# The first six attention tiles computed from key and query columns, one decay table, and another order of loads

## The chip, the cores and the metric

The kernel runs on one core of one Trainium2 chip. The metric is the device time of one execution in microseconds, the median of three runs. A profile of one further execution is read beside it.

## The reference, cut to what matters

Three layers follow each other, all in float32:

```python
# r, k, v: (4, 8, 768, 48); w, u: (8, 48)
for t in range(768):
    cur = einsum('bhd,bhe->bhde', u * k[t], v[t])
    y[t] = einsum('bhd,bhde->bhe', r[t], state + cur)
    state = w[:, :, None] * state + einsum('bhd,bhe->bhde', k[t], v[t])
x = y as (3072, 384)
h = x @ w_in                      # (384, 2048)
x = (h - tanh(h)) @ w_out         # (2048, 384)
# top-1 mixture of 8 experts: cosine logits against expert_emb over tau,
# softmax weight of the best expert, relu(x @ w1[e]) @ w2[e]
```

## The kernel before, in words

The 3072 tokens are 24 attention tiles of 128 tokens. Tile n is batch n % 4, piece n // 4 of its sequence, so tiles 0 to 3 are the first pieces of the four batches (no state goes in) and tiles 4 and 5 second pieces. Three tiles make one token group of 384; group j passes the FFN in 16 steps f of 128 hidden units. All large products are made as three float32r products of high and low parts.

An attention tile (class Att, lines 317 to 429) has its operands twice: r and k as columns (RT and KT, 112 x 4 x 128, tile `tt`: two heads of 48 stacked at partitions 0 and 64) and r, k and v as rows (128 tokens; v padded to 512 columns). The host lays both out. Steps of a tile: `decay_r` and `decay_k` multiply RT and KT by the tables tab_r and tab_k (powers of w, and inverse powers). `bonus` makes r*k*u from the rows in two GpSimd operations, `sums` reduces it over each head's 48 numbers on VectorE into cd. `diagonal` puts cd on the diagonals of two masks `am` (8 ScalarE operations on the identity). `scores` multiplies KT by RT on TensorE, 16 products. `causal` copies the scores above the diagonal into `am` on VectorE. `values` multiplies v and am on TensorE (32 products), `result` splits the outcome into high and low parts of the FFN's input xt (ScalarE, VectorE). `decayed` multiplies the key rows by ktab on GpSimd, a table by rows that `decay_rows` turns out of tab_k; `state_product` and `state_add` make the state for the next tile of the batch.

The weights of the FFN, 64-bit floats in memory, come in 16 pieces of 768 KB in the order w_in, w_out, w_in, ... Each is packed to float32 on VectorE by six bit operations (`convert`, lines 228 to 255) and then split by ScalarE (high) and GpSimd (low) in `split` (line 257). A piece of w_in serves two FFN steps. Pieces of w_out also give router columns: `Logits.turn` (turns by TensorE), `product`, `back`. A raw piece lies in one of seven buffers (STAGE, line 208); `load_next` asks for the next piece once its buffer's previous user is done. Every load is issued on SyncE's one queue, in order.

The startup (lines 137 to 1158) is ordered by hand: inside `manual_schedule` the instructions keep the written order on each engine. There tiles 0 to 2 are computed and pieces 0 to 2 packed. After it comes a loop over 22 steps (lines 1211 to 1258): FFN steps 0 to 5 of group 0, then all 16 of group 1. In the meantime tiles 3 to 5 are made (`attention_stage`, begun at steps 0, 1 and 2) and the remaining pieces packed (at the steps of CONV). From there on a planner with its own cost estimates orders the instructions, and it may also put instructions of the loop between those of the startup. A second part finishes group 0 and does groups 2 to 7 with their tiles, and the experts follow. `store_x` writes a group's columns to memory for a rare path; `routing_table` initializes a table in memory; `embedding_norms`, `embedding_rows`, `embedding_columns` normalize the expert embeddings (a power on GpSimd, then VectorE, then a turn).

PSUM has eight banks, one pool for all tiles named `ps`.

```python
a[2].causal()                        # startup, line 1134
a[2].values()
a[1].result()
ops = convert_next()
for i in range(2):
    for _ in range(3):
        next(ops)
    split(*ready[0], i=i)
```

Of the kernel before, what the change touches and what calls it, by code (L numbers as in the profile page):

```python
# [24 lines left out]
LZ = 0.04  # L25
# [4 lines left out]
def rwkv__then__tanh_ffn__then__top1_moe_kernel(  # L30
# [55 lines left out]
    CONV = (1, 2, 3, 5, 6, 7, 8, 9, 11, 12, 13, 15, 18)  # L86
# [52 lines left out]
    wc = const.tile([PW, HP, 1], F32, name="wc")  # L139
    nc.vector.memset(wc, 0.5)  # L140
# [21 lines left out]
    nc.vector.tensor_copy(out=tri16, in_=strict)  # L162
    sb_t = const.tile([P, 1], F32, name="sb_t")
    nc.vector.memset(sb_t, SB)
    lz_t = const.tile([P, 1], F32, name="lz_t")
    nc.vector.memset(lz_t, -LZ)
    half = const.tile([P, TB], F32, name="half")
    nc.vector.memset(half, 0.5)
    zx = const.tile([P, NB * NF], F32, name="zx")
    ent = const.tile([P, NK, EP], F32, name="ent")  # L170
    nc.vector.memset(ent, 0.0)
# [4 lines left out]
    pw = const.tile([PW, HP, 8], F32, name="pw")  # L176
    w64 = pw[:, :, 6:7]
    w128 = pw[:, :, 7:8]
    rw64 = const.tile([PW, HP, 1], F32, name="rw64")
# [3 lines left out]
    def decay_tables():  # L183
        nc.vector.tensor_copy(out=pw[:, :, 0:1], in_=wc)
        for i in range(7):
            nc.vector.tensor_tensor(out=pw[:, :, i + 1:i + 2], in0=pw[:, :, i:i + 1], in1=pw[:, :, i:i + 1],
                                    op=ALU.mult)
        nc.vector.reciprocal(out=rw64, in_=w64)
        nc.vector.tensor_copy(out=tab_r[:, :, 0:1], in_=rw64)
        nc.vector.tensor_copy(out=tab_k[:, :, P - 1:P], in_=rw64)  # L190
        for i in range(7):
            n = 1 << i
            f = pw[:, :, i:i + 1].to_broadcast([PW, HP, n])
            nc.vector.tensor_tensor(out=tab_r[:, :, n:2 * n], in0=tab_r[:, :, 0:n], in1=f, op=ALU.mult)
            nc.vector.tensor_tensor(out=tab_k[:, :, P - 2 * n:P - n], in0=tab_k[:, :, P - n:P], in1=f, op=ALU.mult)

    def decay_rows():
        pse = ps.tile([P, HP, PW], F32, tag="p", name="ps_tab")
        for q in range(HP):
            nc.tensor.transpose(pse[:, q, :], tab_k[:, q, :], ident[:PW, :PW])  # L200
        for g in range(2):
            nc.scalar.activation(out=ktab.rearrange("p (q g) d -> p g q d", g=2)[:, g],
                                 in_=pse[:, :, 64 * g:64 * g + D], func=AF.Copy)


    CW = 2 * P

# [9 lines left out]
    def load_win(c, t):  # L217
        t = t.rearrange("p (k f) -> p k f", k=NK)
        cols = slice(c * CW, (c + 1) * CW)
        nc.sync.dma_start(out=t, in_=w_in.rearrange("(k p) f -> p k f", p=P)[:, :, cols])  # L220
# [1169 lines left out]
```

## Time and profile before

| | |
|---|---|
| median of 3 runs | 821.34 us (819.63 to 821.76) |
| profiled execution | 822.99 us, span 821.3 us |
| TensorE busy | 775.1 us, 94% |
| VectorE / ScalarE / GpSimd busy | 512.1 / 446.6 / 301.8 us |
| mean granted clock of TensorE | 0.963 |

The span is the profiled time from the first instruction to the last; the execution has 1.7 us around it. A matmul's end is modelled, so a busy TensorE is not one at its peak. The granted clock is a share of 2.4 GHz: 0.50 is 1.2 GHz.

### The profile page before, as it was taken

Reading aid. Unit: us, or ns where it says so; the run is one execution under the profiler, and the core shown is the slowest. Engines: PE = TensorE matmul, PEld = TensorE weight load, DVE = VectorE, ACT = ScalarE, POOL = GpSimd, SP = SyncE. Lnnn points to the kernel's source line nnn. Section 1 sums busy time; section 2 is a strip of 40 time slices with the busy share of each in tenths; the row PEclk is TensorE's granted clock in tenths of the full one; section 3 lists DMA queues with packets and bytes.
Section 4 is the critical chain, followed back from the end, with each engine's and each line's share of the span. In section 5 each row is a group of like instructions: output and inputs, shape, how many; then the busy total and the mean of one; then the engine's idle time right before and its main releaser. Section 6 shows DMA issues by size and latency. Waiting matters only on the chain. (4 is left out here: it accounts for less than half of the span.)

```text
span 821.3 us, 15368 instructions
## 1 busy us (share of the span) xinstructions
PE 775.1 (94%) x5835; PEld 726.9 (89%) x5835; DVE 512.1 (62%) x1092; ACT 446.6 (54%) x1032; POOL 301.8 (37%) x311
## 2 busy tenths in 40 slices
PE   6579999989999999999999999999899999999992
PEld 3468989879999999999989999998889999999992
DVE  6887977666865776775766784756544445454510
ACT  3356676645566656656547666776343434544421
POOL 6563461176541551551561440142331314331111
PEclk7759999999999999999999999999989999999996
DMA  8862621133222222223213201150633335544300
GB/s 275 267 200 94 225 89 39 53 88 114 85 77 91 86 62 106 85 59 111 84 56 113 84 2 58 32 182 30 194 129 121 125 116 185 172 153 152 116 28 30
DMA packets 41446, 89.69 MB, mean 109 GB/s; under 512 B 9329, under 2 KB 21025, under 8 KB 40339
## 3 DMA queue, kind: packets, MB, share of 16 engines
q1 hardware_dynamic: 37042, 79.10, 29.6%
q0 software_dynamic: 4320, 9.51, 3.6%
q8 instruction: 48, 0.79, 0.5%
q14 instruction: 36, 0.29, 0.1%
HBM read 69.82 MB, written 19.47 MB: 109 GB/s over the span
## 5 line engine op out<-in xcount | busy, mean ns | idle before, releaser
L475 PE MATMUL ph<-xt,wq 128*128 128x384 f32 (+2 forms) x1712 | 346.4, 345 | 3.0 <-DVE glo L540 2.5
L475 PEld LDWEIGHTS ph<-xt,wq 128*128 128x128 f32 x1712 | 307.7, 191 | 8.1 <-DVE glo L540 3.4
L486 PE MATMUL acc<-wq,ghi 128*128 128x392 f32 (+2 forms) x1120 | 288.1, 344 | 0.2 <-ACT ghi L553 0.2
L486 PEld LDWEIGHTS acc<-wq,ghi 128*128 128x128 f32 (+1 forms) x1120 | 200.3, 187 | 6.5 <-issue 1.4
L486 PE MATMUL acc<-wq,glo 128*128 128x392 f32 (+2 forms) x560 | 184.9, 342 | 0.5 <-DVE glo L540 0.5
L524 ACT ACTIVATE z<-ph 128x384 f32<-128x384 f32 x128 | 62.6, 489 | 86.2 <-PE ph L475 84.8
L486 PEld LDWEIGHTS acc<-wq,glo 128*128 128x128 f32 (+1 forms) x560 | 103.9, 187 | 1.9 <-DVE glo L540 0.8
L535 ACT ACTIVATE ghi<-ph 128x384 fp32r<-128x384 f32 x128 | 62.6, 490 | 70.2 <-DVE ph L534 62.9
L533 DVE TENSOR_TENSOR ph<-ph,z 128x384 f32<-128x384 f32 x128 | 71.7, 561 | 40.8 <-ACT z L524 40.4
L540 DVE TENSOR_TENSOR glo<-ph,ghi 128x384 fp32r<-128x384 f32 x128 | 71.0, 555 | 41.1 <-ACT ghi L535 39.9
L709 POOL DMA_INDIRECT out_dram<-ob,gts x27 | 28.7, 1063 | 155.1 <-ACT ob L787 149.6
L525 ACT ACTIVATE q<-z,sb_t 128x384 f32<-128x384 f32 x128 | 78.9, 617 | 3.5
L534 DVE SCALAR_TENSOR_TENSOR ph<-q,ph 128x384 f32<-128x384 f32 x128 | 71.7, 561 | 11.3 <-ACT q L525 2.5
L554 DVE SCALAR_TENSOR_TENSOR glo<-ph,ghi 128x384 fp32r<-128x384 f32 (+2 forms) x56 | 31.5, 564 | 74.7 <-ACT ghi L553 65.4
L537 ACT ACTIVATE mk<-z,lz_t 128x384 bf16<-128x384 f32 x128 | 77.1, 602 | 0.0
L553 ACT ACTIVATE ghi<-ph 128x384 fp32r<-128x384 f32 (+2 forms) x56 | 27.7, 496 | 72.8 <-PE ph L475 70.7
L756 DVE TENSOR_TENSOR wq<-eraw,wq 128x768 fp32r<-128x768 f32 x60 | 55.5, 964 | 18.5 <-ACT wq L755 16.9
L755 ACT ACTIVATE wq<-eraw 128x768 fp32r<-128x768 f32 x64 | 50.5, 837 | 12.9 <-DMA eraw<-in_moe_w_dram 12.9
L340 POOL TENSOR_TENSOR rk<-rkv 128x384 f32<-128x384 f32 x22 | 22.6, 1026 | 94.0 <-DMA xs<-xr 64.6
L259 POOL TENSOR_TENSOR wq<-wraw,wq 128x768 fp32r<-128x768 f32 (+1 forms) x17 | 30.2, 1774 | 45.2 <-ACT wq L258 45.2
L332 POOL TENSOR_TENSOR tt<-tt,tab_k 112x512 f32<-112x512 f32 x20 | 34.4, 1721 | 26.5 <-DMA tt<-in_cols_dram 21.3
L355 POOL TENSOR_TENSOR am<-ident,cd 128x512 f32<-128x512 f32 x36 | 36.9, 1047 | 10.6 <-DVE cd L345 10.6
(270 smaller groups left out, 891.4 us busy)
## 6 DMA issues: line engine op xcount, KB each, us to landing
eraw<-in_moe_w_dram SPq DMA_DIRECT2D x32, 768.0 KB
rkv<-in_rows_dram SPq DMA_DIRECT2D x22, 640.0 KB
tt<-in_cols_dram SPq DMA_DIRECT2D x22, 448.0 KB
xd<-xt SPq DMA_DIRECT2D x8, 1152.0 KB
wraw<-in_moe_w_in_dram SPq DMA_DIRECT2D x8, 768.0 KB
wraw<-in_moe_w_out_dram SPq DMA_DIRECT2D x8, 768.0 KB
xs<-xr SPq DMA_DIRECT2D x21, 192.0 KB
first<-in_rows_dram SPq DMA_DIRECT2D x1, 640.0 KB
```

The source lines that it names most:

```text
L355: nc.gpsimd.tensor_tensor(out=a, in0=ident[:, None, :].to_broadcast([P, HP, P]), in1=self.cd[:, :, g:g + 1].to_broadcast([P, HP, P]), op=A ...
L475: nc.tensor.matmul(out=ph, lhsT=lhs[a][:, kk, :], rhs=rhs(b, kk), start=(kk == 0 and p == 0), stop=(kk == nk - 1 and p == 2))
L486: mm = nc.tensor.matmul(out=acc[t], lhsT=g[a][:, t * P:t * P + m], rhs=rhs(b, i), start=(i == span[0] and p == 0), stop=(i == span[1] - 1 ...
L524: nc.scalar.activation(out=z, in_=ph, func=AF.Square)
L525: nc.scalar.activation(out=q, in_=z, func=AF.Square, scale=SS, bias=sb_t)
L533: nc.vector.tensor_tensor(out=ph, in0=ph, in1=z, op=ALU.mult)
L534: nc.vector.scalar_tensor_tensor(out=ph, in0=q, scalar=KC, in1=ph, op0=ALU.add, op1=ALU.mult)
L535: mark["z"] = nc.scalar.activation(out=ghi, in_=ph, func=AF.Copy).ins
L537: nc.scalar.activation(out=mk, in_=z, func=AF.Relu, bias=lz_t, accum_out=zx[:, step:step + 1])
L540: nc.vector.tensor_tensor(out=glo, in0=ph, in1=ghi.bitcast(F32), op=ALU.subtract)
L755: nc.scalar.activation(out=hi[c][:, a], in_=t[:, a], func=AF.Copy)
L756: engs[s % len(engs)].tensor_tensor(out=lo[c][:, a], in0=t[:, a], in1=hi[c][:, a].bitcast(F32), op=ALU.subtract)
```

## The change

For tiles 0 to 5 only v is loaded as rows (256 KB in place of 640 KB). r*k comes from the columns in one operation (`products`: VectorE for tiles 0 to 2, GpSimd for 3 to 5), before the decays; `summed` multiplies it on TensorE by `u_pair`, u as columns with zeros for the other head, and ScalarE copies the sums to cd. The decayed key rows come from the decayed columns: `turned` turns them on TensorE into a bank, `turned_rows` copies them out on ScalarE. Tiles 6 to 23 are as before. tab_k is no longer built by doublings: ScalarE copies tab_r backwards. w goes straight into the table of powers; w and u are asked for on ScalarE's queue.

Loads on SyncE: tiles 0, 1, 2, the embedding and tau, then five weight pieces, then tiles 3, 4, 5, then u as rows. Before: tile 0, u, embedding, tau, tiles 1, 2, three pieces, the routing table, tile 3, a fourth piece, tile 4, further pieces, tile 5. `store_x` and `routing_table` now come behind the last weight load asked for by then (the mark before was a ScalarE instruction, which a load on SyncE doesn't follow). In the startup the clears of the state tiles, the embedding's norms, the constants and the routing's iotas come after tiles 0 to 2; piece 2 is packed in the loop's step 0 instead of the startup.

```diff
-    CONV = (1, 2, 3, 5, 6, 7, 8, 9, 11, 12, 13, 15, 18)
+    CONV = (0, 1, 2, 3, 5, 6, 7, 8, 9, 11, 12, 13, 15, 18)
...
     for g in range(2):
-        nc.sync.dma_start(out=wc[64 * g:64 * g + D, :, 0],
-                          in_=w.rearrange("(q g) d -> g d q", g=2)[g])
+        nc.scalar.dma_start(out=pw[64 * g:64 * g + D, :, 0], in_=w.rearrange("(q g) d -> g d q", g=2)[g])
+    for g in range(2):
+        nc.scalar.dma_start(out=u_pair[64 * g:64 * g + D, :, g], in_=u.rearrange("(q g) d -> g d q", g=2)[g])
...
+        for i in range(6):
+            square(i)
+        nc.vector.reciprocal(out=tab_r[:, :, 0:1], in_=w64)
         for i in range(7):
             n = 1 << i
-            f = pw[:, :, i:i + 1].to_broadcast([PW, HP, n])
-            nc.vector.tensor_tensor(out=tab_r[:, :, n:2 * n], in0=tab_r[:, :, 0:n], in1=f, op=ALU.mult)
-            nc.vector.tensor_tensor(out=tab_k[:, :, P - 2 * n:P - n], in0=tab_k[:, :, P - n:P], in1=f, op=ALU.mult)
+            if i == 5:
+                between()
+            nc.vector.tensor_tensor(out=tab_r[:, :, n:2 * n], in0=tab_r[:, :, 0:n],
+                                    in1=pw[:, :, i:i + 1].to_broadcast([PW, HP, n]), op=ALU.mult)
+        nc.scalar.activation(out=tab_k, in_=tab_r[:, :, ::-1], func=AF.Copy)
+        square(6)
...
+            if n < 2 * TB:
+                rows = rows[:, :HP * P] if n < TB else rows[:, RKV - HP * P:]
         nc.sync.dma_start(out=tt, in_=cols_in[n])
-        nc.sync.dma_start(out=rows, in_=rows_in[n * P:n * P + P, :])
+        nc.sync.dma_start(out=rows, in_=rows_in[n * P:n * P + P, (2 * DM if n < 2 * TB else 0):])
...
+        def turned(self):
+            pse = ps.tile([P, HP, P], F32, tag="p", name="ps_k")
+            for q in range(HP):
+                nc.tensor.transpose(pse[:, q, :PW], self.KT[:, q, :], ident[:PW, :PW])
+            self.pk = pse
+
+        def turned_rows(self):
+            self.ktok = work.tile([P, H, D], F32, name="ktok")
+            nc.scalar.activation(out=self.ktok, in_=self.pk.rearrange("p q (g d) -> p (q g) d", g=2)[:, :, :D],
+                                 func=AF.Copy)
+
+        def products(self, eng):
+            i = self.n % 2 + 1
+            self.rkc = rows5[:PW, i * HP * P:(i + 1) * HP * P].rearrange("p (q t) -> p q t", q=HP)
+            eng.tensor_tensor(out=self.rkc, in0=self.RT, in1=self.KT, op=ALU.mult)
+
+        def summed(self):
+            pc = ps.tile([P, HP, 2], F32, tag="p", name="ps_cd")
+            for q in range(HP):
+                nc.tensor.matmul(out=pc[:, q, :], lhsT=self.rkc[:, q, :], rhs=u_pair[:, q, :], start=True, stop=True)
+            self.cd = work.tile([P, HP, 2], F32, name="cd")
+            nc.scalar.activation(out=self.cd, in_=pc, func=AF.Copy)
...
     def store_x(j, xt):
-        with tc.issue_after(mark["z"]):
+        with tc.issue_after(mark["w"]):
...
     def routing_table():
-        for i in range(2):
+        with tc.issue_after(mark["w"]):
+            for i in range(2):
...
+    for n in range(TB):
+        load_rkv(n)
     nc.sync.dma_start(out=en, in_=emb)
     nc.sync.dma_start(out=tau_t, in_=tau.to_broadcast([P, 1]))
-    load_rkv(1)
-    load_rkv(2)
-    load_next(3)
+    load_next(5)
```

The startup after the loads, as it now stands (its lines of the diff joined):

```python
decay_tables(lambda: a[0].products(nc.vector))
a[0].summed(); a[0].decay_r(nc.vector); a[0].decay_k(nc.vector)
a[0].scores(range(HP)); a[0].diagonal(True); a[0].turned()
a[1].products(nc.vector); a[1].decay_r(nc.vector); a[1].decay_k(nc.vector)
a[1].summed(); a[1].scores(range(HP)); a[1].diagonal(True); a[1].turned()
a[0].causal(); a[0].values()
a[2].products(nc.vector); a[2].decay_r(nc.vector); a[2].decay_k(nc.vector)
a[2].summed(); a[2].scores(range(HP))
a[1].causal(); a[0].result()
a[2].diagonal(True); a[2].turned()
a[1].values()
load_rkv(3); load_rkv(4); load_rkv(5)
# u as rows, small_constants(), two packing steps of piece 0
a[2].causal(); a[2].values()
# one packing step, first half's split
a[1].result()
# three packing steps, second half's split
a[2].result()
a[0].turned_rows(); a[1].turned_rows()
for x in st:
    nc.gpsimd.memset(x, 0.0)
a[0].state_product(); a[1].state_product()
embedding_norms(); embedding_rows(); embedding_columns()
decay_rows(); load_next()
convert_now(); split(*ready[1])
a[2].turned_rows()
nc.vector.tensor_copy(out=tri16, in_=strict)
routing_constants()
```

In `attention_stage` tiles 3 to 5 do `products` and `decay_k` on GpSimd in their first stage, then `summed`, `scores`, `turned`, `diagonal` and `turned_rows` in the second; `decayed` is gone.

## Rows read from the trace of the kernel before

**Rows 1.** The page's slices, forty over the whole span: TensorE's busy tenths

```profile
PE   6579999989999999999999999999899999999992
```

**Rows 2.** Windows: stretch, length, busy us (instructions) by engine; clock, DMA share, GB/s

```profile
10.00:15.00 5.00, 3.02 (x20) 2.44 (x20) 1.98 (x5) 3.37 (x12) 0.75 (x2) 0.50 1.02 349
...
20.00:25.00 5.00, 5.00 (x84) 4.19 (x86) 3.58 (x6) 3.67 (x13) 2.61 (x3) 0.63 0.70 229
...
45.00:50.00 5.00, 2.56 (x28) 1.79 (x28) 2.07 (x4) 3.69 (x10) 2.45 (x3) 0.76 0.82 273
...
60.00:150.00 90.00, 89.53 (x688) 79.44 (x689) 70.03 (x151) 60.72 (x149) 32.80 (x22) 0.97 0.32 104
```

**Rows 3.** In order of time, VectorE, start to 33: start us, busy us, what

```profile
3.83 1.38 DVE L186 TENSOR_TENSOR pw<-pw 112x4 f32<-112x4 f32 x7
...
7.06 0.42 DVE L194 TENSOR_TENSOR tab_r<-tab_r,pw 112x256 f32<-112x256 f32 x1
...
9.14 1.48 DVE L332 TENSOR_TENSOR tt<-tt,tab_k 112x512 f32<-112x512 f32 x1
...
10.54 0.54 DVE L345 TENSOR_REDUCE cd<-rk 128x8 f32<-128x384 f32 x1
...
14.16 0.67 DVE L329 TENSOR_TENSOR tt<-tt,tab_r 112x512 f32<-112x512 f32 x1
...
18.43 1.33 DVE L371 COPY_PREDICATED am<-cmask,pa 128x512 f32<-128x512 uint8 x2
...
27.64 0.55 DVE L245 TENSOR_SCALAR bits<-wraw 128x384 int32<-128x384 int32 x1
...
32.02 0.56 DVE L402 TENSOR_TENSOR xt<-py,xt 128x384 fp32r<-128x384 f32 x1 [0.99 <-ACT xt L401]
```

**Rows 4.** In order of time, TensorE's matmuls, start to 128

```profile
10.67 2.08 PE L366 MATMUL pa<-tt 48*128 48x128 f32 x16 [3.14 <-DVE tt L332]
...
12.68 1.01 PE L200 MATMUL ps_tab<-ident,tab_k 112*128 112x112 f32 x4
...
19.26 2.58 PE L396 MATMUL py<-am,rkv 128*32 128x128 f32 x32 [1.69 <-issue]
...
23.78 1.08 PE L396 MATMUL py<-am,rkv 128*32 128x128 f32 x32
...
35.22 2.81 PE L475 MATMUL ph<-xt,wq 128*128 128x384 f32 x9
...
44.90 1.16 PE L366 MATMUL pa<-tt 48*128 48x128 f32 x16
...
60.03 3.25 PE L475 MATMUL ph<-xt,wq 128*128 128x384 f32 x9 [0.27 <-ACT wt L274]
...
127.94 0.63 PE L272 MATMUL pt<-ident,wraw 128*128 128x128 f32 x4
```

**Rows 5.** In order of time, GpSimd and ScalarE, start to 52

```profile
2.14 1.63 POOL L1103 MEMSET st<- 128x384 f32 x4
...
3.73 1.98 POOL L1080 IOTA tokid<- 128x2 int32 x24
...
11.11 2.45 ACT L353 ACTIVATE am<-ident,cd 128x128 f32<-128x128 f32 x8 [8.92 <-DVE cd L345]
...
14.31 1.57 POOL L1056 TENSOR_TENSOR en_n<-en_n,half 8x1 f32<-8x1 f32 x1 [4.25 <-DVE en_n L1055]
...
31.97 1.01 POOL L259 TENSOR_TENSOR wq<-wraw,wq 128x384 fp32r<-128x384 f32 x1
...
40.46 0.92 ACT L258 ACTIVATE wq<-wraw 128x768 fp32r<-128x768 f32 x1 [1.73 <-DVE wraw L251]
...
47.87 1.78 POOL L332 TENSOR_TENSOR cols<-cols,tab_k 112x512 f32<-112x512 f32 x1 [2.55 <-DMA cols<-in_cols_dram]
...
49.60 1.86 POOL L259 TENSOR_TENSOR wq<-wraw,wq 128x768 fp32r<-128x768 f32 x1
```

**Rows 6.** Waits of SyncE's queue, 0 to 65: in total us, times, longest

```profile
SPq L310 <- PE pst L410: 12.5, 2, 10.6
```

More of the change, by code (lines that the diff above doesn't have):

```diff
@@ L197, in decay_rows @@
+        nc.scalar.activation(out=tab_k, in_=tab_r[:, :, ::-1], func=AF.Copy)
+        square(6)
     def decay_rows():
-        pse = ps.tile([P, HP, PW], F32, tag="p", name="ps_tab")
+        pse = ps.tile([P, HP, P], F32, tag="p", name="ps_tab")
         for q in range(HP):
[L200 to L203, printed above, removed]
+            nc.tensor.transpose(pse[:, q, :PW], tab_k[:, q, :], ident[:PW, :PW])
@@ L298, in load_rkv @@
         if n == TB - 1:
-            t = work.tile([P, 2 * HP * P + RKV], F32, name="first", tag="xt")
+            t = work.tile([P, 2 * HP * P + HP * P], F32, name="first", tag="xt")
             tt = t[:PW, :2 * HP * P].rearrange("p (a q t) -> p a q t", a=2, q=HP)
@@ L1102, in rwkv__then__tanh_ffn__then__top1_moe_kernel @@
-    for t in st:
-        nc.gpsimd.memset(t, 0.0)
-    routing_constants()
-    a[0].bonus(nc.gpsimd)
+    decay_tables(lambda: a[0].products(nc.vector))
+    a[0].summed()
     a[0].decay_r(nc.vector)
     a[0].decay_k(nc.vector)
-    a[0].sums()
+    a[0].scores(range(HP))
     a[0].diagonal(True)
-    a[0].scores(range(HP))
-    embedding_norms()
-    a[1].bonus(nc.gpsimd)
+    a[0].turned()
+    a[1].products(nc.vector)
     a[1].decay_r(nc.vector)
     a[1].decay_k(nc.vector)
-    a[1].sums()
@@ L1116, in rwkv__then__tanh_ffn__then__top1_moe_kernel @@
-    decay_rows()
+    a[1].summed()
+    a[1].scores(range(HP))
     a[1].diagonal(True)
-    a[1].scores(range(HP))
+    a[1].turned()
     a[0].causal()
     a[0].values()
-    a[2].bonus(nc.gpsimd)
+    a[2].products(nc.vector)
     a[2].decay_r(nc.vector)
     a[2].decay_k(nc.vector)
-    a[2].sums()
+    a[2].summed()
     a[2].scores(range(HP))
+    a[1].causal()
+    a[0].result()
     a[2].diagonal(True)
-    a[1].causal()
+    a[2].turned()
     a[1].values()
-    a[0].result()
-    a[1].decayed()
@@ L1131, in rwkv__then__tanh_ffn__then__top1_moe_kernel @@
-    a[1].state_product()
     load_rkv(3)
-    load_next(4)
+    load_rkv(4)
+    load_rkv(5)
+    nc.sync.dma_start(out=u_bc, in_=u.rearrange("(o h) d -> o h d", o=1).to_broadcast([P, H, D]))
+    small_constants()
+    ops = convert_next()
+    for _ in range(2):
+        next(ops)
     a[2].causal()
     a[2].values()
+    next(ops)
+    split(*ready[0], i=0)
     a[1].result()
-    ops = convert_next()
-    for i in range(2):
-        for _ in range(3):
-            next(ops)
-        split(*ready[0], i=i)
@@ L1142, in rwkv__then__tanh_ffn__then__top1_moe_kernel @@
-    done.add(0)
-    a[0].decayed()
+    for _ in ops:
+        pass
+    split(*ready[0], i=1)
+    done.add(0)
+    a[2].result()
+    a[0].turned_rows()
+    a[1].turned_rows()
+    for x in st:
+        nc.gpsimd.memset(x, 0.0)
     a[0].state_product()
-    load_rkv(4)
-    load_next()
-    load_rkv(5)
-    a[2].result()
+    a[1].state_product()
+    embedding_norms()
     embedding_rows()
     embedding_columns()
+    decay_rows()
+    load_next()
     convert_now()
     split(*ready[1])
-    a[2].decayed()
@@ L1154, in rwkv__then__tanh_ffn__then__top1_moe_kernel @@
-    a[1].state_add()
-    convert_now()
-    split(*ready[2])
-    done.add(2)
+    a[2].turned_rows()
+    nc.vector.tensor_copy(out=tri16, in_=strict)
+    routing_constants()
     startup.close()
@@ L1168, in attention_stage @@
             if i == first:
-                t.bonus(nc.gpsimd)
+                t.products(nc.gpsimd)
                 t.decay_k(nc.gpsimd)
@@ L1172, in attention_stage @@
             elif i == first + 1:
-                t.sums()
+                t.summed()
+                t.scores(range(HP))
+                t.turned()
                 t.diagonal(DACT)
-                t.scores(range(HP))
+                t.turned_rows()
             elif i == first + 2:
```

76 lines of the change are left out of this document (37 added, 39 removed).

## The prediction

> **What bounds the kernel now.** I read the page's slices first. TensorE is at nine tenths or more in nearly every slice except the first three [rows 1], and from 60 to 150 us it is busy 89.53 of 90 us with VectorE only 70.03 busy [rows 2]. So the long part is TensorE's own work, the sum of its matmuls, and a microsecond saved before it fills up comes off the end one for one, unless the change adds matmuls. There is no other lever: the chain of waits names only the last scatter. What can move is the start, and I read it by windows, then in order of time, engine by engine.
>
> At the start TensorE is busy 3.02 us of 10 to 15 at a granted clock of 0.50, and the clock is at 0.63 over 20 to 25, where it worked all 5 us [rows 2]. The first FFN product stands at 35.22 us, and only from 60.03 does TensorE run without gaps [rows 4]. The first product waits for two things: the third column block of the first token group (VectorE's line 402, at 32.02 for 0.56, so 32.58) [rows 3] and the second half of the first weight piece's low part (GpSimd's line 259, at 31.97 for 1.01, so 32.98) [rows 5]. Both are ends of VectorE's in-order queue: the bit packing of that weight piece does not begin before 27.64 [rows 3], because three attention tiles stand ahead of it. From 33 to 60 the packing of the next pieces goes on; there the longest hole is 45 to 50: VectorE is busy 2.07 us, idle 2.9, and GpSimd too waits there 2.55 us, for the columns of tile 5 [rows 2, 5]. That transfer is late because SyncE's queue stood 10.6 us behind one load of rows that waited for a state product [rows 6], with weight pieces and later tiles queued behind it.
>
> **The change, part by part.** My measure is the moment at which both inputs of the first product are there (32.98 now): gain A. Then the stretch to a full TensorE: gain B. Then work added to a TensorE that is already full: loss C.
>
> A, *tables*. The squares begin at 3.83 and seven took 1.38; six take 1.2, so 5.0. Reciprocal 0.2. One table instead of two: five doublings, which shrink from the largest at 0.42; I take 0.2 for each, so 6.2. The products r*k of tile 0 now stand here: one 112x512 operation without GpSimd beside it, 0.67 [rows 3], so 6.9. Two last doublings 0.7, so 7.6. The mirror is one ScalarE copy of 512 columns, a form that the trace does not show: below by half of, above by the whole of the 768-column copy at 0.92 [rows 5]; I take two thirds, 0.6, so 8.2. The decay of r runs beside it; the decay of k adds 0.67: 8.9. Now that operation ends at 9.14 + 1.48 = 10.62, because GpSimd's bonus products run beside it [rows 3]. They go, and with them the 0.54 us reduction per tile and the wait of the diagonal for them. So tile 0 is 1.7 us earlier.
>
> The loads of w and u go to ScalarE's queue, which has nothing else to do then; if a table load is put ahead of them, w lands later. I count 0 for it and leave it to the range.
>
> *Tiles 0 to 2*. Per tile VectorE now has products, two decays (3 x 0.67 = 2.0), the causal copies (1.33) and a low part (0.56) [rows 3]; ScalarE a small copy of about 0.2, the diagonal (2.45) and a high part (half of 0.92) [rows 5]; TensorE scores (2.08 at the lower clock, 1.16 at the upper), four turns of keys (1.01 lower; four of a wider form took 0.63 upper), four sums over two columns each, and values (2.58 lower with waits, 1.08 upper) [rows 4]. The sums have no row: between 0.1 and 0.66 (they load weights like the turns but stream 2 columns instead of 112); I take 0.6 lower, 0.3 upper. TensorE per tile: 6.3 lower, 3.2 upper.
>
> Walk at the upper clock: scores of tile 0 at 8.9 to 10.1; diagonal to 10.8; VectorE finishes tile 1's three operations at 10.9, copies tile 0 to 12.2, tile 2's three to 14.2, tile 1's copies to 15.5, tile 0's low part 16.1, two packing steps (0.55 each) to 17.6; tile 2's diagonal ends at 16.9, its copies at 18.9; third packing step 19.5; ScalarE's half and the high part 20.6; low part 21.1; three packing steps 22.9; split and high part 23.9; low part, and GpSimd's 1.01, 24.5. At the lower clock TensorE is the late one: scores, turns, sums, scores, turns of tiles 0 and 1 end at 15.8, values 18.0, sums and scores of tile 2 at 20.8, its diagonal at 21.9, and the same tail gives 28.6. TensorE works here with fewer pauses than it does now, so I take the middle, 26.5: A = 33.0 - 26.5 = 6.5, from 4.4 to 8.5.
>
> By the Trainium skill ("TensorE: Matmul & The Clock Gate", What's actually happening) the throttled state is the default and sustained activity releases it; the trace agrees (0.50 at 10 to 15 with pauses, TensorE busy throughout when it rises). By that rule alone I would have taken 24.5.
>
> B. Taken away: three reductions (3 x 0.54, 1.6) [rows 3], the 2.9 us hole (the columns of tile 5 are asked for right behind five weight pieces and two tiles, with no blocked load ahead), and GpSimd's bonus and key products, three operations a tile, beside which VectorE's two-input operations grow from 0.67 to 1.48. Added: the norms of the embedding now come late. Their power on GpSimd (1.57) stands behind the last split and four clears (1.63) [rows 5], so it ends near 26.5 + 3.2 = 29.7, and VectorE's packing of the second piece stands behind it. VectorE has some 2 us of other work to fill in there: a loss of 0 to 3, I take 1.5. A cast and memsets that moved here cost up to 1. Sum: 1.6 + 2.9 - 1.5 - 1 = 2. Ends: -1 if the hole only changes its place (ScalarE's or GpSimd's order then sets the pace), +5 with nothing lost.
>
> C. Turns and sums of tiles 3 to 5: 0.6 + 0.3 = 0.9 us a tile at the upper clock. Tile 3 comes before TensorE is full, two tiles after: 1.8 (0.9 to 2.7). The write of the first token group's columns and of the routing table move behind weight loads, past the loads of tiles 3 to 5 on SyncE's queue, which only gain by it, and the transfers end up where the DMA engines are mostly idle (60 to 150: share 0.32) [rows 2]: 0.
>
> Sum: 6.5 + 2 - 1.8 = 6.7. The profiled execution took 822.99 (span 821.3, so 1.7 around it), 1.65 over the median of 821.34; a difference carries over unchanged: 821.34 - 6.7 = 814.6.
>
> **The rivals.** *Everything pays*: upper clock through tiles 0 to 2, no wait for the norms: 8.5 + 5 - 0.9 = 12.6, so 808.7. For it: VectorE has the only dense queue and loses work. Against: TensorE's clock was low through 10 to 20. The page named above would make this the forecast.
>
> *TensorE becomes the bound of the start*: the clock stays low, three tiles of 6.3 us in a row, the norms cost their full wait: 4.4 - 0.5 - 1.8 = 2.1, so 819.2. For it: its clock now, and half as much small work again for it. Against: fewer pauses.
>
> *Slower: GpSimd's queue.* It must pass four clears (1.63), the power (1.57), the second piece's split (1.86), the routing constants (1.98 for 24 of 29 iotas, so near 3) and two 112x512 operations for each of tiles 3 to 5 (up to 1.78 each) before or around the third piece's split (1.86) [rows 5]. All of it ahead of that split makes 20.6 us. From 28.6 on this ends at 49.2; if it also stands, in order, for tile 5's columns as it does now (2.55) [rows 5], at 51.8 against 51.46 now. From 51.46 on it decides: the third product is then no earlier than today, the added matmuls (1.8) remain and each further wait counts: near 824. For it: this queue sets the third product now. Against: it loses the bonus work, and nothing blocks the load of those columns any more.
>
> By the Trainium skill ("SBUF — State Buffer", Who interferes with whom) a VectorE instruction with two SBUF inputs and a GpSimd one that reads SBUF exclude each other for a whole instruction; the 1.48 against 0.67 agrees, and the new products on GpSimd are of that kind, which speaks for this rival.
>
> *It does not do what it says*: the later steps' order eats what the start gives, for instance accumulation held back by banks that the turned keys occupy until late: about 821.
>
> **How the numbers follow.** Chances: forecast 0.42 (own range 812 to 817), everything pays 0.22, TensorE bound 0.18, no effect 0.09, slower 0.09. About 0.3% (2.5 us) is what a measurement tells from no change. Faster takes the first two and half of the third: 0.73. Same: the other half and no effect, 0.18. Slower 0.09. The range 807 to 820.5 leaves out some tenth on each side.
>
> **What would show it.** Right: the first line-475 product between 24 and 30; no 10 us wait on SyncE before the fourth weight piece; VectorE's two-input operations of tiles 0 to 2 near 0.67; tile 5's columns landed before 35; TensorE without gaps from about 52; some 2 us more of small matmuls after that. Wrong: a first product after 33; GpSimd's third split after 50; scores of tiles 1 and 2 waiting for TensorE at 0.50; VectorE idle for over 3 us behind the embedding's power. A time over 819 would refute the sum, one under 809 its caution on the clock and the norms.

## The result, and the profile after

The changed kernel took 829.45 us (median of five runs; 827.46 to 830.13) against 821.34 for the kernel before in the same session: ratio 1.0098 [1.0076, 1.012], slower. Timed again on another chip it was 825.19 (822.06 to 829.18) against 822.00: 1.004 [1.0016, 1.0064]. The forecast was 814.6, and its range ended at 820.5. So about 7 us were forecast as a gain and 3 to 8 came as a loss.

The profiled execution of the changed kernel took 829.45 (span 827.8, so 1.7 around it, as before). The page's slices of TensorE:

```profile
PE   8489999989999999999999999999899999999992
```

Against [rows 1] the first slice rose from 6 to 8, the second fell from 5 to 4, the third rose from 7 to 8, and the long part is as full as it was. The windows of [rows 2]:

```profile
10.00:15.00 5.00, 4.49 (x29) 4.18 (x29) 4.67 (x8) 3.19 (x10) 0.00 (x0) 0.50 1.05 387
20.00:25.00 5.00, 4.00 (x76) 3.25 (x64) 0.80 (x2) 2.88 (x10) 2.04 (x2) 1.00 1.05 300
45.00:50.00 5.00, 4.74 (x61) 4.12 (x60) 3.70 (x9) 5.00 (x12) 4.18 (x30) 1.00 0.19 34
60.00:150.00 90.00, 89.05 (x690) 78.32 (x690) 69.61 (x150) 59.72 (x147) 31.81 (x21) 0.96 0.35 118
```

From 10 to 15 TensorE and VectorE are far busier than before, and the hole from 45 to 50 is gone (VectorE 3.70 against 2.07 us): both were forecast. The reader should stop at 20 to 25: VectorE, whose queue the forecast walked through without a pause, is busy 0.80 of 5 us, while the DMA engines are full (1.05). VectorE in order of time shows why:

```profile
6.15 1.17 DVE L187 TENSOR_TENSOR pw<-pw 112x4 f32<-112x4 f32 x6 [3.88 <-DMA pw<-in_w_dram]
...
10.60 0.69 DVE L342 TENSOR_TENSOR tt<-tt,tab_k 112x512 f32<-112x512 f32 x1
...
24.20 0.69 DVE L339 TENSOR_TENSOR tt<-tt,tab_r 112x512 f32<-112x512 f32 x1 [4.87 <-POOL rows L360]
24.81 0.55 DVE L438 TENSOR_TENSOR xt<-py,xt 128x384 fp32r<-128x384 f32 x1
...
25.42 0.54 DVE L251 TENSOR_SCALAR bits<-wraw 128x384 int32<-128x384 int32 x1
28.39 0.69 DVE L339 TENSOR_TENSOR tt<-tt,tab_r 112x512 f32<-112x512 f32 x1 [2.43 <-POOL rows L360]
...
35.41 0.56 DVE L438 TENSOR_TENSOR xt<-py,xt 128x384 fp32r<-128x384 f32 x1 [0.99 <-ACT xt L437]
```

The squares start at 6.15 instead of 3.83 [rows 3], behind w. At 24.20 and 28.39 stand the decays of r (line 339) of tiles 3 and 4. They belong to the loop, not to the hand-written start, but the planner put them into VectorE's queue ahead of tile 0's low part (24.81) and between the packing steps of the first weight piece. Each overwrites columns that GpSimd's product r*k (line 360) must have read, and GpSimd waits for those columns:

```profile
22.89 1.28 POOL L360 TENSOR_TENSOR rows<-tt 112x512 f32<-112x512 f32 x1 [20.88 <-DMA tt<-in_cols_dram]
...
27.09 1.26 POOL L360 TENSOR_TENSOR rows<-tt 112x512 f32<-112x512 f32 x1 [1.06 <-DMA tt<-in_cols_dram]
...
35.08 1.02 POOL L265 TENSOR_TENSOR wq<-wraw,wq 128x384 fp32r<-128x384 f32 x1 [2.17 <-ACT wq L264]
```

The columns of tiles 3 and 4 were asked for behind five weight pieces of 768 KB. So the chain is five pieces, then columns, then GpSimd's product, then VectorE's decay, and behind that everything in VectorE's order. VectorE's two waits that matter, from 0 to 75 us (in total, times, longest):

```profile
DVE tt L339 <- POOL rows L360: 7.3, 2, 4.9
DVE pw L187 <- DMA pw<-in_w_dram: 3.9, 1, 3.9
```

Of the first of these waits 2.6 us would have passed idle anyhow: tile 0's low part, next in VectorE's order, needs ScalarE's high part, which ended at 21.96, and VectorE had nothing left since 19.34:

```profile
21.48 0.48 ACT L437 ACTIVATE xt<-py 128x384 fp32r<-128x384 f32 x1
```

Both inputs of the first product are there at 35.41 + 0.56 = 35.97 and 35.08 + 1.02 = 36.10 (32.98 before, 26.5 forecast). TensorE:

```profile
11.34 2.08 PE L402 MATMUL pa<-tt 48*128 48x128 f32 x16 [0.51 <-DVE tt L342]
13.35 1.01 PE L348 MATMUL ps_k<-ident,tt 112*128 112x112 f32 x4
14.15 1.73 PE L366 MATMUL ps_cd<-u_pair,rows 112*128 112x2 f32 x8
...
20.31 1.05 PE L366 MATMUL ps_cd<-u_pair,rows 112*128 112x2 f32 x8
...
30.23 2.53 PE L432 MATMUL py<-am,first 128*32 128x128 f32 x32 [6.23 <-DVE am L407]
...
39.22 0.45 PE L1099 MATMUL ps_en<-ident,en 8*128 8x8 f32 x3 [1.89 <-DVE en L1094]
...
40.29 3.23 PE L511 MATMUL ph<-xt,wq 128*128 128x384 f32 x9
...
52.42 1.49 PE L511 MATMUL ph<-xt,wq 128*128 128x384 f32 x7 [1.06 <-POOL wq L265]
...
62.58 1.32 PE L522 MATMUL acc<-wq,ghi 128*128 128x392 f32 x3 [0.58 <-DVE am L407]
```

Against [rows 4] the scores of tile 0 come 0.7 us later (11.34), not 1.8 earlier, and the first product at 40.29 against 35.22. The sums (line 366) are x8: four products are recorded as eight matmuls, 1.73 us at the granted clock of 0.50 and 1.05 at the upper one.

To see what of this reaches the end I follow one event through all kernels: the start of the square of the same FFN step on ScalarE (in the last two rows a high part of the experts), each kernel minus the kernel before, in their profiled executions (us; each column is one execution, and that of before took 822.99, 1.65 over its median). The repaired kernels are e1, e7, e8 timed again and e13 of the next section:

| FFN step, time before | changed | changed, other chip | order repaired | loads repaired | three repairs | three repairs and tile 5 held |
|---|---|---|---|---|---|---|
| 0, at 46.07 | -2.5 | -2.7 | -7.0 | -6.5 | -9.0 | -12.2 |
| 2, at 55.10 | -1.1 | -1.3 | -5.5 | -4.8 | -5.6 | -8.9 |
| 3, at 63.31 | +1.5 | +1.3 | -2.9 | -2.1 | -5.4 | -8.9 |
| 5, at 77.12 | +3.0 | +1.1 | -2.2 | -2.4 | -4.4 | -7.6 |
| 20, at 143.67 | +2.1 | +0.2 | -3.1 | -3.3 | -5.3 | -8.5 |
| 96, at 448.54 | +2.7 | -1.0 | -4.3 | -3.2 | -5.1 | -8.8 |
| experts, at 617.70 | +6.1 | +0.6 | -0.7 | +0.8 | -3.4 | -8.2 |
| near the end, 801.58 | +6.4 | +0.9 | -0.5 | +1.2 | -3.0 | -7.8 |

One execution against one is coarse: b1, whose time is that of the kernel before, stands at -2.6 at step 5 in the same count. So a single difference under some 3 us tells nothing; what recurs from column to column does. Each of two repairs moves step 5 by some 5 us against the changed kernel, so what they take away is made before step 5.

Two more differences recur. From step 2 to step 3 the first four columns lose 2.6 or 2.7 us, the last two 0.2 and none. In those four one decay on VectorE takes 3.57 or 3.58 us (shown below for the changed kernel, at 55.45), in the last two the longest takes 2.38 and 2.37, and the next packing, ScalarE's split and the square of step 3 stand behind it; no run tests this by itself. And 1 to 4 us are lost around 580 to 612 in most kernels of the changed family. There ScalarE's split of expert weights waits longer for them (before, then the changed kernel):

```profile
583.08 1.58 ACT L755 ACTIVATE wq<-eraw 128x768 fp32r<-128x768 f32 x2 [3.46 <-DMA eraw<-in_moe_w_dram]
```

```profile
588.37 1.58 ACT L787 ACTIVATE wq<-eraw 128x768 fp32r<-128x768 f32 x2 [5.33 <-DMA eraw<-in_moe_w_dram]
```

A high part stands behind that split in ScalarE's order, and TensorE waits 2.1 us for it (0.2 before). Why the weights land later stays open.

### The profile page after: what moved, and what is told of

Its sections match the earlier page's. It is cut to its first block, busy times and chain, and to the rows that moved or that the text cites. A ratio compares the mean times of both kernels' runs of the same rounds, so it can differ in the third digit from the quotient of the medians.

```text
span 827.8 us, 15511 instructions
## 1 busy us (share of the span) xinstructions
PE 783.1 (95%) x5907; PEld 735.1 (89%) x5907; DVE 506.7 (61%) x1080; ACT 450.4 (54%) x1044; POOL 285.1 (34%) x296
## 5 line engine op out<-in xcount | busy, mean ns | idle before, releaser
L568 DVE SCALAR_TENSOR_TENSOR ph<-q,ph 128x384 f32<-128x384 f32 x128 | 71.7, 561 | 12.2 <-ACT q L559 3.6
L376 POOL TENSOR_TENSOR rk<-rkv 128x384 f32<-128x384 f32 x18 | 18.3, 1018 | 93.4 <-DMA xs<-xr 45.5
L391 POOL TENSOR_TENSOR am<-ident,cd 128x512 f32<-128x512 f32 x36 | 37.4, 1062 | 12.2 <-DVE cd L381 12.2
```

The lines of the kernel that those rows point to most:

```text
L391: nc.gpsimd.tensor_tensor(out=a, in0=ident[:, None, :].to_broadcast([P, HP, P]), in1=self.cd[:, :, g:g + 1].to_broadcast([P, HP, P]), op=A ...
L568: nc.vector.scalar_tensor_tensor(out=ph, in0=q, scalar=KC, in1=ph, op0=ALU.add, op1=ALU.mult)
```

## The experiments

All edits but those of the three kernels named b1 to b3 are made to the changed kernel; the code shows the lines that matter. Ratios are to the kernel before on the same chip, with 95% intervals.

### What holds up VectorE: the order, or w, or the norms

**e1**, the order: tiles 3 to 5's decays of r are held behind tile 2's low part.

```
-  later.append(lambda t=t: t.decay_r(nc.vector))
+  def late(t=t):
+      with tc.issue_after(mark[TB - 1]):   # tile 2's low part
+          t.decay_r(nc.vector)
+  later.append(late)
```

> The changed kernel with one edge more: the decays of r of tiles 3 to 5 on VectorE come only behind the low part of tile 2. Theory A (VectorE's order): in the changed kernel these decays stood ahead of the low part of tile 0 and VectorE waited 4.87 and 2.43 us for tile 3's and tile 4's products, which wait for columns behind five weight pieces. Then no such wait is left, both inputs of the first FFN product are there at about 31 us in place of 36.1, and the time falls from 829.4 to about 824.5. Theory C (TensorE at its lower clock carries the start): VectorE then waits for TensorE or ScalarE instead, the inputs come at 34 or later, and the time stays within 1.5 us of 829.4. Theory B (late table of powers) and theory D (embedding norms ahead of the first product) expect no change by this edge.

Measured 821.04, ratio 0.9997 [0.9976, 1.0018]: the loss is gone, VectorE waits for no product of GpSimd, and both inputs of the first product are there at 31.19, as theory A said (31). The time fell further than its 824.5.

**e2**, w: `nc.scalar.dma_start(out=pw...)` becomes `nc.sync.dma_start`, first in SyncE's queue.

> The changed kernel with w asked for first on SyncE's queue, as before the change, and u still on ScalarE's. Theory B (w lands late because it shares the DMA engines with the tile loads from another queue): the squares begin near 3.8 us in place of 6.15, tile 0's decayed keys are ready near 9 in place of 11.3, and the time falls by 2.3 to 827. Theory A: the squares begin as early as that, but VectorE's wait for tile 3's columns takes it all: that wait grows from 4.87 to about 7, and the time stays at 829.4 within 1 us.

Measured 824.48, ratio 1.0031 [1.001, 1.0052]. The squares wait 1.6 us, not 3.9; VectorE's wait for GpSimd's products stays, 7.8 us. Earlier work only runs sooner into the same wall.

**e3**, the norms: `embedding_norms()` stands between tiles 0 and 1.

> The changed kernel with the embedding's norms (square on ScalarE, maximum on VectorE, power on GpSimd) put back between tiles 0 and 1, where GpSimd is idle; the rest of that chain stays. Theory D (the first product stands on TensorE behind the turn of the embedding, which waits for the power): the first product begins near 38 us in place of 40.3 and the time falls by 2, to 827.5. Theories A, B and C: what follows is set by VectorE's packing of the next pieces; the time moves by less than 1 us.

Measured 824.68, ratio 1.0043 [1.002, 1.0066], as the changed kernel itself on the second chip (825.19). The first product did begin at 38.07, as theory D said, but nothing of it is left at the end.

**e4**, the three together.

> The three edits together. If A, B and D each hold and add up: both inputs of the first product near 28 to 29 us, the first product near 31, the time 829.4 - 5 - 2.3 - 2 = about 820, a little under the kernel before. If TensorE's lower clock and added work carry the start (C): inputs at 33, time 826 or more.

Measured 821.73, ratio 0.9997 [0.9979, 1.0015]: no better than the order alone. GpSimd's 5.1 us of work for tiles 3 and 4 now stood ahead of the first piece's low parts in GpSimd's own order, and the inputs were there at 32.76.

**e5**, e4 with GpSimd's work for tiles 3 to 5 held behind the first piece's second low part, and the embedding's rows moved ahead.

> The kernel of e4 with two edits more: GpSimd's work on tiles 3 to 5 comes only behind the second low part of the first weight piece (in e4 5.1 us of it stood in front of that part, which ended at 32.8), and the embedding's rows are normalized between tiles 0 and 2, its turn and that of the decay table behind the second piece's split. If GpSimd's queue and the embedding are what e4 still loses: inputs of the first product at 30.5 in place of 32.8, the first product at 32 in place of 35.7, the time 3 us under e4, 818.5. If VectorE's packing of the next pieces or TensorE's added work sets what follows: the first product comes as early, but the fifth one no earlier than in e4, and the time stays within 1 us of 821.7.

Measured 821.56, ratio 0.9999 [0.9981, 1.0017]. The first product came at 32.03, as the first alternative said, and the first square 11.1 us earlier than in the kernel before; step 2 came 2.8 us later and step 5 only 0.9 earlier. What was held back seems to come due at step 2. An earlier first product alone was worth nothing.

**e6**, TensorE's added work: e1, with the sums of tile 0 used for all six tiles.

```
 def summed(self):
+    if self.n > 0:
+        self.cd = a[0].cd
+        return
```

> The kernel of e1 without TensorE's sums of r*k*u for tiles 1 to 5: the sums of tile 0 are used in their place, so this leaves out 20 of the 24 small products and five copies of 0.18 us on ScalarE. Theory C (TensorE's added work is what the change costs; four sums took 1.87 at the lower and 1.05 at the upper clock): tiles 1 and 2 give 3.7 us at the lower clock on the path of the start, tiles 3 to 5 some 3 us at the upper, so 5 to 6.5 us less than e1: 815 to 816. If VectorE's queue carries the start after e1: 2 tiles at full TensorE, 1.5 to 2 us, 819.

Measured 821.57, ratio 0.9995 [0.9978, 1.0012]: the same as e1. In its one profiled execution step 5 comes 3.1 us earlier than in e1's, as much as three sums at the upper clock; the medians show nothing of it.

### Who makes the columns late: five pieces at once

**e7**, the loads: two pieces, tiles 3 and 4, three pieces, tile 5.

```
-  load_next(5)                      # before the start
+  load_next(2)
...
   load_rkv(3); load_rkv(4)
+  load_next(5)
   load_rkv(5)
```

> The changed kernel with only two weight pieces asked for at once; tiles 3 and 4 come next, then three pieces, then tile 5. The order on VectorE stays that of the planner. Theory A in its other form (what hurt is that tile 3's columns stand behind five pieces): they land at about 17 in place of 22.9 and tile 4's at about 20 in place of 27, VectorE's waits of 4.87 and 2.43 us shrink under 1.5 in total, and the time falls by 5 to 7 us, to 823, as with e1. If the dependence on GpSimd's product makes the wait, not the transfer: over 3 us of waits stay and the time stays over 826.

Measured 819.89, ratio 0.997 [0.9952, 0.9987]: some 2.5 us faster than before, and 5.3 under the changed kernel on the same chip. Neither alternative came whole: the decay of tile 4 no longer waits for GpSimd, tile 3's still does, 3.4 us, and the time fell all the same.

**b1**, the kernel before with the store of the token columns and the routing table behind weight loads, as the change has them.

> The kernel before with one part of the change alone: the store of a group's columns and the routing table come behind the weight loads asked for by then. Forecast of the prediction: nothing, within 1 us. If that part makes the 2 to 4 us that the changed kernels lose where the experts begin (between 580 and 612 us TensorE waits 2.1 us for ScalarE in each of them, 0.2 before): that wait appears here too and the time rises by 2 to 3 us.

Measured 822.50, ratio 1.0008 [0.9989, 1.0028]: this part of the change does nothing that these runs can tell. (The call that writes the routing table also moves from step 0 of the loop to step 4, as in the change.)

**b2**, the kernel before with five pieces asked for at once.

```
-    load_next(3)
+    load_next(5)
 ...
     load_rkv(3)
-    load_next(4)
```

> The kernel before with only the five weight pieces asked for at once (three, then one more later, before). If the burst of loads alone costs time (the columns of tile 3 then land behind five pieces, some 9 us later than behind three): 823 to 825 us. If it costs only together with VectorE's wait on GpSimd's products, which the kernel before doesn't have (its decays of r for tile 3 wait for nothing of GpSimd): 821 to 822.5 us, no difference. I expect the second.

Measured 828.05, ratio 1.0084 [1.0066, 1.0101]: I expected no difference and was wrong. One part of the change put into the kernel before costs 6 us. The wall stands there on GpSimd, whose rows in order of time are:

```profile
29.14 1.71 POOL L332 TENSOR_TENSOR tt<-tt,tab_k 112x512 f32<-112x512 f32 x1 [5.84 <-PE py L396]
...
35.19 1.71 POOL L332 TENSOR_TENSOR tt<-tt,tab_k 112x512 f32<-112x512 f32 x1
...
37.84 1.11 POOL L336 TENSOR_TENSOR ktok<-rkv,ktab 128x384 f32<-128x384 f32 x1
```

and TensorE's:

```profile
39.00 0.88 PE L410 MATMUL pst<-rkv,ktok 128*48 128x48 f32 x16 [9.89 <-POOL ktok L336]
39.81 0.48 PE L1067 MATMUL ps_en<-ident,en 8*128 8x8 f32 x3
40.23 3.25 PE L475 MATMUL ph<-xt,wq 128*128 128x384 f32 x9
```

GpSimd comes to tile 3's columns at 29.14. The wait is put down to TensorE, but VectorE's decay of the same tile, at 29.04, ends a wait for those columns; before, it stood at 24.89. In GpSimd's order the decayed keys of an earlier tile come after both tiles' columns (37.84; 32.94 before), TensorE's state product after them (9.89 us of waiting), and then the first product, at 40.23 against 35.22 [rows 4].

**b3**, the opposite: the kernel before with two pieces instead of three ahead of tile 3.

> The kernel before, with two weight pieces instead of three asked for ahead of tile 3's loads. If the order of the loads alone makes the difference (five cost that kernel 6 us against three): 818 to 820 us, 2 us or more under the kernel before. If tile 3's loads there wait for something else than the third piece (SyncE waits 10.6 us for a buffer of tile 0 that TensorE gives back, rows 6): 821 to 823 us, no difference. I expect the second.

Measured 822.94, ratio 1.0017 [1.0003, 1.0032]: nothing to be won there. Tile 3's loads wait for a buffer in that kernel [rows 6], not for the third piece.

### Putting the repairs together

**a0**, the changed kernel once more.

> The changed kernel once more, untouched, beside the three kernels that follow. All theories: 828 to 830 us, 1.007 to 1.011 of the kernel before; VectorE waits 7.3 us in two places for GpSimd's products of tiles 3 and 4, and 3.9 us for w. It gives the mean that the mended versions of this call are set against.

Measured 825.19, ratio 1.004 [1.0016, 1.0064]. The waits are as expected (7.1 and 3.9), the time lower than I expected.

**e8**, order, loads and w; timed twice.

> Three repairs together: w first on SyncE's queue, the decays of r of tiles 3 to 5 held until tile 2's low part, and tiles 3 and 4 asked for after two weight pieces instead of five. Theory A (VectorE's order with GpSimd's products is the loss, each of two repairs alone takes it all away): no better than the better of the two alone, 820 to 821 us. Theory B (the late w is a loss of its own of 2 us): 817 to 819 us. Theory C (TensorE's added work at the lower clock has taken what was to be won, so mending the start leaves the time of before): 820 to 823 us, with the first steps 5 us or more ahead of before and little of it left at the experts. A and C against B is what this tells.

Measured 817.56, ratio 0.9936 [0.9914, 0.9957].

> The changed kernel with three repairs (w first on SyncE's queue, decays of r of tiles 3 to 5 after tile 2's low part, tiles 3 and 4 asked for after two weight pieces), once more. All theories: 816 to 819 us, 0.992 to 0.997 of the kernel before.

Measured 817.68, ratio 0.9965 [0.9949, 0.9981]. Both times below the order alone and the loads alone, as theory B said. The two ratios differ by 0.3%, so the gain is 3 to 5 us.

**e9**, these three and the norms early.

> As the kernel with three repairs, and the embedding norms' work on VectorE between tiles 0 and 1 instead of after tile 2. Theory D (the norms behind tile 2 hold up the second half of the first product): 1 to 2 us under the kernel with three repairs. Theory C: the same time as that kernel within 1 us, 820 to 823 us, since what the start wins isn't kept. I expect the second.

Measured 819.17, ratio 0.9978 [0.996, 0.9995], 1.6 us above e8 on the same chip: moving the norms ahead gains nothing.

**e10**, e8 without w's repair.

> Two repairs, order and loads; w is still asked for on ScalarE's queue. Theory B (the late w, 3.9 us of VectorE's wait against 1.6, holds up the first products by 2.3 us and the end by as much): 2 us above the kernel with three repairs, 819 to 821 us. Rival (the first tiles have slack behind TensorE's slow stretch, so w's place is worth nothing): the same within 0.8 us, 816.5 to 818.5. I expect the first.

Measured 819.53, ratio 0.998 [0.9962, 0.9998], 1.9 us above e8 on the same chip (1.2 by the two ratios, whose intervals overlap): the sign and size that I expected for the late w, once the order lets it show, though not sharply measured.

**e11**, e8 without the sums of tiles 1 to 5 (the edit of e6).

> Three repairs, and TensorE's sums computed for tile 0 alone and used for tiles 1 to 5 as well; this leaves out 20 of the 24 small products and five copies of their result. Theory C (TensorE's added work stands on the path of a start that is mended): 2 of the sums stand at the lower clock and 3 at the upper, 2 x 1.8 + 3 x 1.05 = 6.7 us of TensorE, of which those ahead of TensorE's full stretch are partly covered: 2.5 to 4.5 us under the kernel with three repairs, 813 to 815 us. Rival (what the start wins is taken back later, as where the start wasn't mended): the same within 1 us.

Measured 823.29, ratio 1.0019 [0.9995, 1.0043]: 5.6 us slower with less work. VectorE and TensorE of that kernel in order of time:

```profile
31.30 0.69 DVE L339 TENSOR_TENSOR cols<-cols,tab_r 112x512 f32<-112x512 f32 x1 [4.24 <-POOL rows L360]
```

```profile
37.02 0.46 PE L1102 MATMUL ps_en<-ident,en 8*128 8x8 f32 x3 [9.80 <-DVE en L1097]
```

The planner, with less to place, put tile 5's decay of r ahead of the embedding's rows; it waits 4.24 us for GpSimd, and TensorE stands 9.80 us behind. The first cause has come back one tile later.

**e13** and **e12**: e8 with tile 5's decay held behind the copy of the embedding's columns, with the sums and without.

```
-  with tc.issue_after(mark[TB - 1]):
+  with tc.issue_after(mark["ent" if t.n == 2 * TB - 1 else TB - 1]):
```

> Three repairs, and tile 5's decay of r held until the copy of the embedding's columns. It ran at 49 us in the kernel with three repairs, well behind that copy (33.4), so nothing should change: 816.5 to 819 us.

Measured 816.31, ratio 0.9945 [0.9927, 0.9963]: with e8 the best of all, 4.5 us under the kernel before by the ratio. The edge changed no order here, so this is in effect e8 a third time.

> The same without TensorE's sums of tiles 1 to 5 (tile 0's are used for all six; 20 of 24 small products and five copies are left out). Theory A (the 5.6 us lost without the sums were tile 5's early decay on VectorE): under 819 us, and no wait of VectorE for a GpSimd product over 2 us. Theory C (the sums' TensorE time stands on the path): 2 to 4.5 us under the kernel with the sums, 813.5 to 816. Rival to C (the sums' time is covered, or what it gives is taken back later): within 1 us of the kernel with the sums. I expect A, and half of C, 816.

Measured 821.78, ratio 0.9999 [0.9983, 1.0015]: 5.5 us slower than e13, without the sums. Of A the wait came true, no decay of VectorE waits for a product any more, but not the time; of C nothing. GpSimd in that kernel, in order of time:

```profile
29.18 1.26 POOL L360 TENSOR_TENSOR rows<-cols 112x512 f32<-112x512 f32 x1 [5.63 <-DMA cols<-in_cols_dram]
...
31.74 1.01 POOL L265 TENSOR_TENSOR wq<-wraw,wq 128x384 fp32r<-128x384 f32 x1
32.69 1.49 POOL L1187 MEMSET st<- 128x384 f32 x4
```

Now tile 5's product is ahead in GpSimd's order and waits 5.6 us for its columns; behind it stand the first piece's second low part (24.14 + 2.44 = 26.58 at its end in e13) and the clearing of the states. VectorE's longest wait for GpSimd is now 4.1 us, for that clearing. A decay held on one engine left the product free to block the other.

## Why the prediction was wrong

**The step that failed is A**, "both inputs of the first product", 26.5 forecast and 36.10 measured, at the place where its walk lists VectorE's queue: three operations a tile for tiles 0 to 2, the causal copies, low parts, packing, and nothing else. Two things were missing from it.

First, the decays of r of tiles 3 and 4, 7.3 us of waiting. The trace of before showed them. These rows of VectorE in the kernel before stood in no group of mine:

```profile
24.89 0.69 DVE L329 TENSOR_TENSOR tt<-tt,tab_r 112x512 f32<-112x512 f32 x1 [1.42 <-DMA tt<-in_cols_dram]
...
34.07 0.67 DVE L329 TENSOR_TENSOR tt<-tt,tab_r 112x512 f32<-112x512 f32 x1
```

That is a loop instruction of tile 3 in the middle of the hand-written start, already waiting for its columns. I had read SyncE's queue only for tile 5's columns ("right behind five weight pieces and two tiles, with no blocked load ahead") and did not price those two tiles, which now stood behind five pieces. e1 and e7, which change only the order or only the loads, each take the loss away.

Second, w, "I count 0 for it": the squares began at 6.15 instead of 3.83, 2.3 us. e10 against e8 shows 1.2 to 1.9 us of that at the end.

With both added, and less the 2.6 us that would have been idle anyhow, the forecast's walk at the lower clock gives 28.6 + 7.3 - 2.6 + 2.3 = 35.6; measured 36.10. The rest of the walk was nearly right, as the repaired kernels show, which have neither. Their start is the same; e13 ran 10 to 20 us at a clock of 1.00, e8 timed again at 0.50. Of e13:

```profile
3.89 1.17 DVE L187 TENSOR_TENSOR pw<-pw 112x4 f32<-112x4 f32 x6 [1.62 <-DMA pw<-in_w_dram]
...
15.82 0.56 DVE L438 TENSOR_TENSOR xt<-py,xt 128x384 fp32r<-128x384 f32 x1 [0.47 <-ACT xt L437]
```

```profile
22.57 0.55 ACT L264 ACTIVATE wq<-wraw 128x384 fp32r<-128x384 f32 x1 [2.28 <-DVE wraw L257]
```

```profile
22.92 1.27 POOL L342 TENSOR_TENSOR tt<-tt,tab_k 112x512 f32<-112x512 f32 x1
24.14 2.44 POOL L265 TENSOR_TENSOR wq<-wraw,wq 128x384 fp32r<-128x384 f32 x2
```

```profile
9.08 1.16 PE L402 MATMUL pa<-tt 48*128 48x128 f32 x16 [0.63 <-DVE tt L342]
...
30.65 3.23 PE L511 MATMUL ph<-xt,wq 128*128 128x384 f32 x9
```

and of e8 timed again:

```profile
28.30 1.02 POOL L265 TENSOR_TENSOR wq<-wraw,wq 128x384 fp32r<-128x384 f32 x1 [2.45 <-ACT wq L264]
```

e13 is to be held against the walk at the upper clock: scores of tile 0 at 9.08 (8.9), tile 0's low part over at 16.38 (16.1), ScalarE's second high part over at 23.12 (23.5), the first piece's low part at 24.14 + 2.44 = 26.58 (24.5). The last 2 us are the first cause once more: tile 4's keys stand ahead of both low parts in GpSimd's order. At the lower clock the low part was over at 29.32 (28.6). That 26.58 falls on the forecast's 26.5, the middle of two clocks, is chance. By its ratio e13 gained 4.5 us and e8 5.3 and 2.9, where 6.7 were forecast: my sum priced the change without the order of loads that it came with.

**The measure was too narrow.** "The moment at which both inputs of the first product are there" was to count one for one. In e5 the first square came 11.1 us early and the time did not move; in the changed kernel the first square is 2.5 us *earlier* than before though the inputs are 3.1 us later. In the kernel before those inputs, at 32.98, held up neither the product nor its square, which the prediction missed. On TensorE a state product stood ahead, waiting for the decayed keys on GpSimd, which ended at 33.93; and on ScalarE the first square began 8 us after its product had ended (35.22 + 2.81 = 38.03), behind the diagonals of tiles 3 and 4:

```profile
33.98 0.89 PE L410 MATMUL pst<-rkv,ktok 128*48 128x48 f32 x16 [5.48 <-POOL ktok L336]
```

```profile
42.93 2.44 ACT L353 ACTIVATE am<-ident,cd 128x128 f32<-128x128 f32 x8 [1.55 <-DVE cd L345]
...
46.07 0.47 ACT L524 ACTIVATE z<-ph 128x384 f32<-128x384 f32 x1
```

The start has to be measured where TensorE has lost its last gap, near step 5 here.

**B** (+2): the hole from 45 to 50 went, as forecast. The wait behind the norms came too (TensorE stands 1.89 us for the embedding's turn at 39.22), but kernels with the norms early were no faster (e3, e9), so the term (-1.5) was not needed. What the sum lacked is the later start of everything behind A: TensorE runs without gaps from 62.58 against 60.03 before.

**C** (-1.8): the turns were right (1.01 lower, 0.60 upper). The sums, taken as 0.6 and 0.3, take 1.73 to 1.87 and 1.05, outside the stated bounds (0.1 to 0.66). The added TensorE work is 0.60 + 1.05 = 1.65 us a tile at the upper clock, not 0.9, so -3.3 by the forecast's own count of two tiles. What it costs at the end could not be isolated: each removal (e6, e11, e12) let the planner reorder, and two of the three became slower.

**The rivals.** "Slower: GpSimd's queue" had the right sign and engine, and its queue did pass the point given: the third piece's split, behind the routing constants as listed, ended at 52.37 against 51.46 before, and the rest of the third product waited 1.06 us for it. But e1 and e7 keep that wait (1.07) and no longer have the loss, so the loss was made earlier, through VectorE's wait on this queue. "TensorE becomes the bound of the start" was half right: the granted clock was 0.50 over 10 to 15 and TensorE busy 4.49 of 5 us, but then TensorE stood 6.23 us idle for VectorE. (In that rival's sum the full wait for the norms makes B 1.6 + 2.9 - 3 - 1 = +0.5, not -0.5, so 818.2; nothing hangs on it.)

**The two rules weighed there.** TensorE's clock stayed at 0.50 through 10 to 20 us with TensorE busy 9.49 of 10 us, and was 1.00 over 20 to 25. The same start is seen at either level, e8 timed again and then e13:

```profile
10.00:25.00 15.00, 15.00 (x142) 13.11 (x144) 8.97 (x19) 7.07 (x25) 5.28 (x5) 0.50 1.04 331
```

```profile
10.00:20.00 10.00, 9.31 (x162) 7.63 (x158) 8.78 (x19) 7.37 (x26) 2.36 (x2) 1.00 1.04 336
```

By the Trainium skill ("TensorE: Matmul & The Clock Gate", What's actually happening) sustained activity releases the throttle. The changed kernel agrees, later than the 24.5 that I had derived from it needs; e8 does not, where TensorE counts as busy all 15 us and the clock is 0.50 throughout. There the measurement decides: a row's busy time didn't foretell the level. What sets it no run isolates. Between these two executions it goes with 2.7 us at the inputs of the first product (26.58 and 29.32) and 3.2 us at step 5.

The second rule is that of VectorE beside GpSimd. Beside GpSimd's operations at 54.94 and 56.61 one decay on VectorE took 3.57 us, against 0.69 alone:

```profile
55.45 3.57 DVE L339 TENSOR_TENSOR tt<-tt,tab_r 112x512 f32<-112x512 f32 x1
```

By the Trainium skill ("SBUF — State Buffer", Who interferes with whom) these exclude each other for whole instructions, and this agrees: GpSimd's two operations, 1.72 and 1.86 us, ended at 58.47, the decay 0.55 us after them. The prediction counted GpSimd's old products beside VectorE as taken away; the new ones do the same here.

## What to carry to other kernels

Before pricing a change of loads, list for every engine which instructions stand in its order between the change and the end of the start, those of later loop iterations too: the trace of before shows them at their times, and each one's input has to be followed to its place in the DMA queue. One instruction that waits on a late transfer holds all that its engine does after it, and then the engines that wait for those. Count a gain at the start only where the bounding engine has lost its last gap, and expect that taking work away may let a planner move something else into the hole, as it did twice here.

## What the runs showed of the hardware that I had not expected

- Four matmuls of four-byte floats with two columns (recorded as x8) took 1.05 us at the upper clock, the four turns with 112 columns 0.60 and 16 scores with 128 columns 1.16. What sets the price of the small ones no run isolates.
- Two loads of 0.8 KB issued by ScalarE at 1.08 to 1.97 us, beside bulk loads of SyncE, let the squares begin only at 6.15; with w issued first by SyncE, ahead of the bulk loads, they began at 3.89 (e13).
- Over 143 runs of the kernel before (818 to 828 us) the time falls with the mean granted clock of TensorE, 0.959 to 0.973: correlation -0.66, 3.6 us for each 0.01. The repaired kernels ran at a higher mean (0.972 to 0.974, before 0.966), which by that slope is 2 to 3 us of their gain of 3 to 5; whether the clock is a cause of it or comes with a denser start was not tested.
